# Decay attention feeding two gated MLPs: the order of the first weight loads, and where the state's decay is computed

## The chip, the cores and the metric

The kernel runs on one NeuronCore of a Trainium2 chip. The metric is device time in microseconds (us), the median of several executions. TensorE (PE) does the matrix products, VectorE (DVE), ScalarE (ACT) and GpSimd (POOL) the elementwise work, and SyncE (SP) issues every DMA, in program order, on one queue.

## The reference

Everything is float32: decayed linear attention with a running state, then two MLPs without a softmax or an activation table.

```
attention, batch 2, heads 8, sequence 768, head_dim 64, for each head with its decay lam:
    out_i = sum_{j<=i} lam^(i-j) (q_i . k_j) v_j        (written with blocks of 64 and a state kv)
x = out as 1536 tokens x 512
x = ((x @ w_a) * (x @ w_b)) @ w_out                      w_a, w_b: 512 x 1536
out = max(x @ w1, x @ w2, x @ w3) @ w_out2               w1, w2, w3: 512 x 768
```

## The kernel before, in words

The kernel uses blocks of 128 tokens (C = 128), so there are 6 blocks (`c`) for each of the 2 batches (`b`): twelve steps n = 0 to 11 in `order`. For step n, `load` brings queries and keys into the tile `aq` (issue L385, 512 KB) and keys and values into `av` (also 512 KB; columns 0 to 511 are keys, 512 to 1023 values). `scores` (L395) multiplies keys by queries into two PSUM banks, `masked` (L418, DVE, two instructions) applies the decay table and frees them, `side` (L405, L408, POOL) scales the queries and the keys for the state, and `values` (L434, L439, L446) takes two more banks `o`: scores by values, queries by state, and keys by values for the new state. After `values`, ACT copies the result into `x` (L190, two instructions), DVE adds the new state (L458 for the first block, L460 later), and multiplies it by the decay of a block into `stt` (L463, 128x256, for c < 4), which the next block of that batch adds.

PSUM has eight banks, handed out in turn by `bank`; a matmul into a bank waits until the earlier tile in it was read.

The weights come as float64 (`wup`, 1024 KB an item). `converted` turns an item into float32: L223 (DVE), L226 (ACT), L228 (DVE), L231 and L233 (ACT), L235 (DVE). Then `up_pair` splits it into a rounded part `hi` (ACT copy, L190) and the rest `lo` (DVE subtract, L187), since every product is done as three products of such parts. Raw items have two buffers (`wr`), so the load of item m + 2 waits until L228 of item m has read its own. In the code before, that load is issued straight behind L228 of item m (`load_to(m + 2)`, L229), and it stands in SP's queue ahead of what is issued later.

The attention output is split in the same manner (`Operands`: x0 for the first three blocks, x1 for the last three; `x0A` are its plain quarters A11, A12, A21, A22, and `x0S` their sums). From n = 7 on, one step of the first MLP (`plain_group`, L552, twelve matmuls into a bank `p`) follows each attention step. Items 0 and 1 serve those; from item 2 on `Group.product` (L534, tiles `zu`, `bu`, `xu`) takes over.

The order on DVE, ACT and POOL is fixed when the program is written, by the planner `Pace`. It keeps a model clock for each engine, advanced by a cost for each instruction; `pace.pe(cost)` moves PE's clock and then `pump` lets tasks (item conversions, operand splits) emit their next instruction if their input and their engine are free, by the model, within 2 us of PE's clock. Tasks with a lower rank come first. A task at a gate waits until the program opens it (`open_to`). On the chip every engine then works through its list strictly in that order, apart from PE's weight loads, and waits where an input is not there.

Of the kernel before, what the change touches and what calls it, by code (L numbers as in the profile page):

```python
# [12 lines left out]
AF = mybir.ActivationFunctionType  # L13
ALU = mybir.AluOpType

B, H, S, D = 2, 8, 768, 64
C = 128
NC = S // C
NP = H // 2
# [15 lines left out]
NPLAIN = 2  # L35
# [127 lines left out]
def decay_attention_gated_mlps(ctx: ExitStack, tc: tile.TileContext, qkv: bass.AP, lam: bass.AP, wup: bass.AP, wdown: bass.AP, out: bass.AP):  # L163
    nc = tc.nc
# [7 lines left out]
    pace = Pace()  # L172
# [27 lines left out]
    def load_to(n):  # L200
        while state["raw"] <= min(n, len(items) - 1):
            m = state["raw"]
            kind, i = items[m]
            t = wp.tile([128, 1024], I64, tag="r", bufs=2, name=f"wr{m}")
            if kind == "up":
                nc.sync.dma_start(out=t, in_=wup[i])
            else:
                nc.sync.dma_start(out=t[:, 0:WB], in_=wdown[i])
            raw[m] = t
            state["raw"] += 1  # L210

    def converted(m, width, roomy=False):

        load_to(m)
        bits = raw.pop(m)[:, 0:width].bitcast(I32).rearrange("p (n two) -> p n two", two=2)
        low, high = bits[:, :, 0], bits[:, :, 1]
        yield ("DVE",), width, "2"
        t = slot(f"wd{m}") if roomy else hp.tile([128, 1792], F32, tag="h", name=f"w{m}")  # L220
        f = t[:, 0:width]
        w = f.bitcast(I32)
        nc.vector.tensor_scalar(out=w, in0=high, scalar1=3, scalar2=0x40000000, op0=ALU.logical_shift_left, op1=ALU.bitwise_xor)  # L223
        yield ("ACT",), width + 60, "S"
        sign = wp.tile([128, width], F32, tag="s", bufs=1, name=f"ws{m}") if width > WB else t[:, WB:2 * WB]
        nc.scalar.activation(out=sign, in_=high.bitcast(F32), func=AF.Identity, bias=bias[:, 0:1])  # L226
        yield ("DVE",), width, "S"
        nc.vector.scalar_tensor_tensor(out=w, in0=low, scalar=29, in1=w, op0=ALU.logical_shift_right, op1=ALU.bitwise_or)  # L228
        load_to(m + 2)  # L229
        yield ("ACT",), width, "S"  # L230
        nc.scalar.activation(out=sign, in_=sign, func=AF.Sign, bias=bias[:, 1:2])  # L231
        yield ("ACT",), width, "S"
        nc.scalar.activation(out=f, in_=f, func=AF.Abs)  # L233
        yield ("DVE",), width, "S"
        nc.vector.tensor_tensor(out=f, in0=f, in1=sign, op=ALU.mult)  # L235
        return t

    wop, wtask = {}, {}
# [60 lines left out]
    def items_to(m):  # L299
        while state["item"] <= min(m, len(items) - 1):  # L300
            n = state["item"]
            kind, i = items[n]
            wtask[n] = pace.opens["done", n] = pace.add((up_pair if kind == "up" else down_block)(n, i), 1 if n > 1 else -1)
            state["item"] += 1

    def open_to(what, m):
        if m < len(items):
            items_to(m)
            pace.open((what, m))
# [20 lines left out]
    ltab = tables_sb[:, 1024:1536].rearrange("p (a i) -> p a i", a=NP)  # L330
# [31 lines left out]
    order = [(b, c) for c in range(NC) for b in range(B)]  # L362
# [14 lines left out]
    def load(n, *which):  # L377

        if n >= len(order):
            return  # L380
        b, c = order[n]
        for i in which:
            of, name = ((aq, "aq"), (av, "av"))[i]
            of[n] = slot(f"{name}{n}")
            nc.sync.dma_start(out=of[n][:, 0:1024], in_=qkv[b * NC + c, i])  # L385

    def scores(n):
        if n >= len(order):
            return
        q, k = aq[n][:, 0:512], aq[n][:, 512:1024]  # L390
        banks = [bank(f"s{n}_{g}") for g in range(2)]
        for h in range(H):
            r, p = rows(h), h // 2
            o = slice(128 * p, 128 * p + 128)
            nc.tensor.matmul(banks[side_of(h)][:, o], k[r, o], q[r, o], start=True, stop=True)  # L395
        sc[n] = banks
        pace.pe(1.1)
# [24 lines left out]
    def values(n):  # L422
        b, c = order[n]
        v, kd, qs = av[n][:, 512:1024], av[n][:, 1024:1536], aq[n][:, 1024:1536]
        ps = [bank(f"o{n}_{s}") for s in range(2)]

        def place(h):
            r, p = 64 * (h % 2), h // 2
            return ps[p % 2][r:r + 64, 128 * (p // 2):128 * (p // 2) + 128]

        for h in range(H):
            p = h // 2
            o = 512 * side_of(h) + 128 * p
            nc.tensor.matmul(place(h), v[:, 64 * h:64 * h + 64], am[n][:, o:o + 128], start=p < 2, stop=False, skip_group_check=True)  # L434
        pace.pe(1.1)
        if c > 0:
            for h in range(H):
                p = h // 2
                nc.tensor.matmul(place(h), sts[b][rows(h), 64 * p:64 * p + 64], qs[rows(h), 128 * p:128 * p + 128], start=False, stop=False, skip_group_check=True)  # L439
            pace.pe(0.65)  # L440
        kv = ps[1][:, 256:512]
        if c < NC - 1:
            for h in range(H):
                p = h // 2
                o = 256 * side_of(h) + 64 * p
                nc.tensor.matmul(kv[rows(h), 64 * p:64 * p + 64], kd[:, o:o + 64], v[:, 64 * h:64 * h + 64], start=False, stop=p == NP - 1, skip_group_check=True)  # L446
            pace.pe(0.65)
        j, r = c // 3, c % 3
        if r == 0:
            xa[j, b] = slot(f"x{j}{b}").rearrange("p (a i) -> p a i", a=KD)  # L450
        for s in range(2):
            copy(xa[j, b][:, s:KD:2, C * r:C * r + C], ps[s][:, 0:256].rearrange("p (a i) -> p a i", a=2))
            pace.run("ACT", 256)
        if c < NC - 1:
            src = kv.rearrange("p (a e) -> p a e", a=NP)
            std = sts[b].rearrange("p (a e) -> p a e", a=NP)
            if c == 0:
                nc.vector.tensor_copy(std, src)  # L458
            else:
                nc.vector.tensor_tensor(out=std, in0=src, in1=stt[b], op=ALU.add)  # L460
            pace.run("DVE", 256)
            if c < NC - 2:
                nc.vector.tensor_tensor(out=stt[b], in0=std, in1=ltab[:, :, C - 1:C].to_broadcast([128, NP, 64]), op=ALU.mult)  # L463
                pace.run("DVE", 256, kind="S")


    def split_part(a, h, l):
# [6 lines left out]
    class Operands:  # L474
# [5 lines left out]
        def __init__(self, a, name, order=ORDER):  # L480
            self.ops, self.name, self.made = {}, name, {}
            a11, a12, a21, a22 = a[0][:, 0:2], a[0][:, 2:4], a[1][:, 0:2], a[1][:, 2:4]
            s12 = slot(f"{name}s12").rearrange("p (s a n) -> p s a n", s=2, a=2)
            s1, s2 = s12[:, 0], s12[:, 1]
            self.sums = {"S1": (s1, a21, a22, ALU.add), "S2": (s2, s1, a11, ALU.subtract), "S3": (a21, a21, a11, ALU.subtract), "S4": (s1, a12, s2, ALU.subtract)}
            self.src = {"A11": a11, "S1": s1, "S2": s2, "A12": a12, "A21": a21, "S3": a21, "A22": a22, "S4": s1}
            self.tasks = {}
            for i, x in enumerate(order):
                t = self.tasks[x] = pace.add(self.make(i, x, "A21" in order), 0)
                for g in ("sum", "part"):  # L490
                    pace.opens[name, g, x] = t

# [201 lines left out]
    with tc.manual_schedule():  # L694
# [6 lines left out]
            nc.gpsimd.memset(bias[:, i:i + 1], (1 - 2 * i) * ROUND)  # L701
        nc.scalar.activation(out=warm[:, 0:1], in_=warm[:, 0:1], func=AF.Copy)
        ps = bank("warm_ps")
        for i in range(9):
            nc.tensor.matmul(ps, warm[:, 0:128], warm, start=True, stop=True)
        powers()
        load(0, 1)
        tables()
# [3 lines left out]
        load(3, 0)  # L712
        load(2, 1)
        pace.t["PE"] = 6.0
        for n in range(3):
            scores(n)
        pace.t["PE"] = 12.0
        for n in range(2):
            masked(n)
            side(n)  # L720
# [47 lines left out]
        for n in range(len(order)):  # L768
            load(n + 4, 0)
            load(n + 3, 1)  # L770
            if n in (1, 4):
                m = n // 4
                open_to("conv", m)
                open_to("split", m)
            if n == 7:
                open_to("conv", NPLAIN)
            if n > 0:
                scores(n + 2)
            side(n + 2)
            masked(n + 2)  # L780
            values(n)
            if n % 6 == 5:
                j = n // 6
                xo[j] = Operands([xa[j, b] for b in range(B)], f"x{j}", Operands.PLAIN)
                for i in range(8):
                    pace.open((f"x{j}", i))
            if n == 10:
                pace.open(("x0", "sums"))
            if n > 6:
                next(layer1)  # L790
# [116 lines left out]
```

## Time and profile before

| | |
|---|---|
| median of 3 runs | 546.04 us (545.58 to 546.85) |
| profiled execution | 545.02 us, its span 543.2 us |
| PE busy | 511.7 us (94%) |
| DVE busy | 377.4 us (69%) |
| ACT busy | 280.7 us (52%) |
| POOL busy | 48.2 us (9%) |
| mean granted TensorE clock | 0.984 |

The span is what the profiler saw of the engines; what lies around it makes the difference to the profiled execution's own time (1.8 us). Times in the rows count from the start of the span. Attention fills the first 70 us or so, the first MLP runs to about 346 us, the second to the end. A granted clock of 1.00 is 2.4 GHz, one of 0.50 is 1.2 GHz.

### The profile page before, as it was taken

The numbers are of one execution on the slowest core, as the hardware profiler recorded it, in microseconds if no ns is written. First come the engines' busy times: TensorE is split into PE (matmuls) and PEld (weight loads), VectorE is DVE, ScalarE is ACT, GpSimd is POOL, SyncE is SP. The second block draws the span as 40 slices with busy tenths as digits, with TensorE's granted clock in tenths as the row PEclk, the third lists the DMA queues.
The fourth block names the chain that finished last, engine by engine and source line by source line (L and its number), as shares of the span: only waits on it lengthen the run. The fifth ranks groups of instructions, "written<-read, shape, count | busy, mean of one in ns | idle before, by whom it ended". The sixth has DMA issues, their size and how long they took to land.

```text
span 543.2 us, 7761 instructions
## 1 busy us (share of the span) xinstructions
PE 511.7 (94%) x3167; PEld 469.3 (86%) x3167; DVE 377.4 (69%) x554; ACT 280.7 (52%) x419; POOL 48.2 (9%) x46
## 2 busy tenths in 40 slices
PE   4886999999999999999899999998999999978997
PEld 2765899999999999997678888798999999966886
DVE  3288888887777777489879069375898989892000
ACT  1163564765555555368887066535665566671111
POOL 1647000011111110111000000000000000000000
PEclk9888999999999999999999999999999999997999
DMA  7985310222222211015452001000222211200111
GB/s 223 406 346 209 122 74 1 78 77 78 78 78 78 77 60 58 2 59 174 151 197 78 1 0 43 36 1 0 78 78 77 80 58 59 83 34 39 59 70 66
DMA packets 11812, 48.49 MB, mean 89 GB/s; under 512 B 1272, under 2 KB 3072, under 8 KB 9088
## 3 DMA queue, kind: packets, MB, share of 16 engines
q1 hardware_dynamic: 11776, 47.99, 24.6%
q8 instruction: 25, 0.41, 0.3%
q14 instruction: 11, 0.09, 0.1%
HBM read 44.83 MB, written 3.15 MB: 88 GB/s over the span
## 4 chain that ended last, share of the span: by engine, by line
PE 77%; DVE 12%; DMA 5%; ACT 4%; issue 1%; SPq 1%; ACTq 0%
PE zu L534 15%; PE yp L657 13%; PE zv L534 11%; PE out L685 9%; PE bu L534 7%; PE p L552 7%; PE bv L534 6%; PE xu L534 4%; PE xv L534 2%; DMA aq<-qkv_dram 2%; DMA wr<-wup_dram 2%; DVE m L594 1%; PE o L434 1%; DVE wd L228 1%; DVE w L228 1%
## 5 line engine op out<-in xcount | busy, mean ns | idle before, releaser
L187 DVE TENSOR_TENSOR lo<-w,hi 128x1024 fp32r<-128x1024 f32 (+1 forms) x40 | 49.1, 1235 | 6.7 <-ACT hi L190 6.7
L190 ACT ACTIVATE hi<-w 128x1024 fp32r<-128x1024 f32 (+1 forms) x40 | 37.3, 953 | 13.3 <-DVE w L187 7.9
L657 PE MATMUL yp<-gh,dh 128*128 128x512 f32 x108 | 42.3, 391 | 1.9 <-ACT dh L190 1.9
L657 PE MATMUL yp<-gh,dl 128*128 128x512 f32 x108 | 42.2, 391 | 0.9 <-DVE dl L187 0.9
L657 PE MATMUL yp<-gl,dh 128*128 128x512 f32 x108 | 42.0, 389 | 0.0
L187 DVE TENSOR_TENSOR gl<-g,gh 128x512 fp32r<-128x512 f32 x36 | 24.7, 700 | 19.3 <-ACT gh L190 19.3
L583 POOL TENSOR_TENSOR g<-z1u,z6u 128x384 f32<-128x384 f32 x20 | 22.1, 1104 | 172.7 <-DVE z6u L565 116.6
L688 DVE COPY ob<-out 128x256 f32<-128x256 f32 x1 | 0.4, 425 | 47.6 <-PE out L685 47.6
L228 DVE SCALAR_TENSOR_TENSOR w<-wr,w 128x1024 int32<-128x1024 int32 (+1 forms) x26 | 31.1, 1196 | 0.5
L235 DVE TENSOR_TENSOR w<-w,ws 128x1024 f32<-128x1024 f32 x21 | 25.7, 1223 | 6.3 <-ACT w L233 6.2
L233 ACT ACTIVATE w<-w 128x1024 f32<-128x1024 f32 (+1 forms) x26 | 26.4, 1014 | 7.1 <-DVE w L228 6.9
L187 DVE TENSOR_TENSOR w<-w 128x256 f32<-128x256 f32 (+1 forms) x57 | 29.1, 510 | 1.2
L226 ACT ACTIVATE ws<-wr,bias 128x1024 f32<-128x1024 f32 x21 | 25.9, 1233 | 5.6 <-DMA wr<-wup_dram 5.6
L190 ACT ACTIVATE ob<-out 128x512 f32<-128x512 f32 (+1 forms) x12 | 7.0, 580 | 39.8 <-PE out L685 39.8
L657 PEld LDWEIGHTS yp<-gh,dh 128*128 128x128 f32 x108 | 20.3, 188 | 6.8 <-ACT dh L190 2.8
L190 ACT ACTIVATE z6u<-zu 128x384 f32<-128x384 f32 x20 | 9.8, 492 | 30.3 <-PE zu L534 30.3
L657 PEld LDWEIGHTS yp<-gh,dl 128*128 128x128 f32 x108 | 20.3, 188 | 6.0 <-DVE dl L187 1.8
L190 ACT ACTIVATE x<-o 128x256 f32<-128x256 f32 x24 | 8.9, 383 | 31.3 <-PE o L434 16.5
L231 ACT ACTIVATE ws<-ws,bias 128x1024 f32<-128x1024 f32 x21 | 24.1, 1148 | 0.3
L657 PEld LDWEIGHTS yp<-gl,dh 128*128 128x128 f32 x108 | 20.3, 188 | 4.1
L418 DVE TENSOR_TENSOR am<-s,tables 128x512 f32<-128x512 f32 x24 | 15.4, 682 | 10.4 <-DMA tables<-tab_d 6.4
L552 PE MATMUL p<-x0A,hi 128*128 128x384 f32 x64 | 18.4, 365 | 4.1 <-DVE x0A L187 4.1
(200 smaller groups left out, 1505.9 us busy)
## 6 DMA issues: line engine op xcount, KB each, us to landing
wr<-wup_dram SPq DMA_DIRECT2D x21, 1024.0 KB, 4.8
wr<-wdown_dram SPq DMA_DIRECT2D x12, 768.0 KB, 4.3
aq<-qkv_dram SPq DMA_DIRECT2D x12, 512.0 KB, 6.4
av<-qkv_dram SPq DMA_DIRECT2D x12, 512.0 KB, 8.5
out_dram<-ob SPq DMA_DIRECT2D x11, 256.0 KB, 2.0
tables<-tab_d SPq DMA_DIRECT2D x4, 128.0 KB, 4.0
tables<-tab_d SPq DMA_DIRECT2D x4, 64.0 KB, 4.4
out_dram<-ob SPq DMA_DIRECT2D x2, 128.0 KB, 1.7
```

Source lines behind the costliest of these rows:

```text
L187: (nc.vector if e == "DVE" else nc.gpsimd).tensor_tensor(out=o, in0=a, in1=b, op=op)
L190: nc.scalar.activation(out=o, in_=a, func=AF.Copy)
L226: nc.scalar.activation(out=sign, in_=high.bitcast(F32), func=AF.Identity, bias=bias[:, 0:1])
L228: nc.vector.scalar_tensor_tensor(out=w, in0=low, scalar=29, in1=w, op0=ALU.logical_shift_right, op1=ALU.bitwise_or)
L231: nc.scalar.activation(out=sign, in_=sign, func=AF.Sign, bias=bias[:, 1:2])
L233: nc.scalar.activation(out=f, in_=f, func=AF.Abs)
L235: nc.vector.tensor_tensor(out=f, in0=f, in1=sign, op=ALU.mult)
L534: nc.tensor.matmul(ps, w, x, start=p in FIRST and i == 0, stop=i == len(todo) - 1, skip_group_check=p not in FIRST)
L552: nc.tensor.matmul(ps, w[:, 128 * k:128 * k + 128], x[:, k], start=m == 0, stop=m == 11)
L583: nc.gpsimd.tensor_tensor(out=ga[g.n][:, tokens(g.j, 0)], in0=g.z[1], in1=g.z[6], op=ALU.mult)
L657: nc.tensor.matmul(ps[e], w[:, cols], g, start=k == 0 and m == 0, stop=k == K1 - 1 and m == 2)
L685: nc.tensor.matmul(ps, a[:, o:o + 128], w[:, s], start=k == 0 and n == 0, stop=k == K2 - 1 and n == 2)
```

## The change

- The loads of items 2 and 3 are no longer issued behind L228 of items 0 and 1, but at n = 9, behind every load of queries, keys and values. Item 0 is loaded and opened for conversion at n = 2 instead of n = 1, item 1 at n = 7 instead of n = 4 (before, its load was issued together with item 2's, behind L228 of item 0), item 2 is opened at n = 9 instead of n = 7.
- For the last block of each batch (c = 5, n = 10 and 11), `av` gets its values only: 256 KB in place of 512.
- The state's decay (L463) moves from DVE, one instruction of 128x256, to ACT, four of 128x64 with a scale for each partition: eight DVE instructions become 32 on ACT.
- `values(0)` is issued ahead of `scores(2)`; before, `scores(2)` stood ahead of the loop.
- Eight more empty matmuls (128x512, bf16, into the bank of the nine at the start) stand behind `scores(1)`.
- Ranks in the planner: item 1 from -1 to 1, item 2 from 1 to 0.5, the tasks of the sums S1 to S4 of x0 and x1 from 0 to 0.7. PE's model clock is set to 11 instead of 12 ahead of the first masks.

```diff
@@ converted
-        load_to(m + 2)
+        if m > 1:
+            load_to(m + 2)
@@ items_to
-            wtask[n] = ... 1 if n > 1 else -1)
+            wtask[n] = ... {0: -1, 2: 0.5}.get(n, 1))
@@ load
-            nc.sync.dma_start(out=of[n][:, 0:1024], in_=qkv[b * NC + c, i])
+            s = slice(512 if i == 1 and c == NC - 1 else 0, 1024)
+            nc.sync.dma_start(out=of[n][:, s], in_=qkv[b * NC + c, i, :, s])
@@ values
             if c < NC - 2:
-                nc.vector.tensor_tensor(out=stt[b], in0=std, in1=ltab[:, :, C - 1:C].to_broadcast([128, NP, 64]), op=ALU.mult)
-                pace.run("DVE", 256, kind="S")
+                for p in range(NP):
+                    nc.scalar.activation(out=stt[b][:, p], in_=std[:, p], func=AF.Copy, scale=ltab[:, p, C - 1:C])
+                    pace.run("ACT", 64)
@@ Operands
-                t = self.tasks[x] = pace.add(self.make(i, x, "A21" in order), 0)
+                t = self.tasks[x] = pace.add(self.make(i, x, "A21" in order), 0.7 if "A21" in order and x[0] == "S" else 0)
@@ ahead of the loop
-        for i in range(9):
-            nc.tensor.matmul(ps, warm[:, 0:128], warm, start=True, stop=True)
+        def keep_warm(n):
+            for i in range(n):
+                nc.tensor.matmul(ps, warm[:, 0:128], warm, start=True, stop=True)
+        keep_warm(9)
...
-        for n in range(3):
+        for n in range(2):
             scores(n)
-        pace.t["PE"] = 12.0
+        keep_warm(8)
+        pace.t["PE"] = 11.0
@@ the loop over n
-            if n in (1, 4):
+            if n in (2, 7):
                 m = n // 4
+                load_to(m)
                 open_to("conv", m)
                 open_to("split", m)
-            if n == 7:
+            if n == 9:
+                load_to(NPLAIN + 1)
                 open_to("conv", NPLAIN)
-            if n > 0:
-                scores(n + 2)
+            if n == 0:
+                values(n)
+            scores(n + 2)
             side(n + 2)
             masked(n + 2)
-            values(n)
+            if n > 0:
+                values(n)
```

## Rows read from the trace of the kernel before

**Rows 1.** Waits of PE from 0 to 72 us: total us, times, longest.
```profile
PE s L395 <- DMA aq<-qkv_dram: 7.0, 4, 4.9
PE p L552 <- DVE x0A L187: 4.1, 1, 4.1
PE o L434 <- DVE stt L458: 2.3, 1, 2.3
```

**Rows 2.** Busy time by stretch: PE, PEld, DVE, ACT, POOL, clock, DMA share, GB/s.
```profile
97.00:236.00 139.00, 139.00 (x803) 138.80 (x802) 105.40 (x151) 75.35 (x107) 19.40 (x18) 1.00 0.19 67
```

**Rows 3.** Timeline of SP's queue, 0 to 130 us: start, length, line, transfer.
```profile
15.86 0.46 SPq L206 DMA_DIRECT2D wr<-wup_dram  x1
...
21.81 11.53 SPq L206 DMA_DIRECT2D wr<-wup_dram  x2
```

**Rows 4.** Busy time by stretches of 2 us, columns as in rows 2.
```profile
28.00:30.00 2.00, 2.00 (x24) 1.67 (x28) 1.97 (x5) 0.62 (x3) 0.73 (x1) 0.50 1.05 420
...
32.00:34.00 2.00, 2.00 (x42) 1.54 (x40) 1.97 (x3) 1.85 (x2) 2.00 (x2) 1.00 0.40 127
```

**Rows 5.** The chain that ended last, 33 to 56 us: start, length, what.
```profile
33.38 6.00 DMA aq<-qkv_dram
...
51.11 3.92 PE p L552 x11
55.03 1.09 PE s L395 x16
```

**Rows 6.** Timeline of all engines, 18 to 30 us.
```profile
18.14 1.16 PE L395 MATMUL s<-aq 64*128 64x128 f32 x16 [0.34 <-DMA aq<-qkv_dram]
...
24.31 1.06 POOL L408 TENSOR_TENSOR av<-av,tables 128x512 f32<-128x512 f32 x1 [0.17 <-DMA av<-qkv_dram]
...
26.77 0.69 DVE L223 TENSOR_SCALAR w<-wr 128x1024 int32<-128x1024 int32 x1 [6.12 <-DMA wr<-wup_dram]
...
27.98 0.64 ACT L190 ACTIVATE x<-o 128x256 f32<-128x256 f32 x2
...
29.27 1.06 POOL L408 TENSOR_TENSOR av<-av,tables 128x512 f32<-128x512 f32 x1 [2.68 <-DMA av<-qkv_dram]
```

**Rows 7.** Groups by form, 0 to 60 us: busy us, mean ns, idle before.
```profile
L418 DVE TENSOR_TENSOR am<-s,tables 128x512 f32<-128x512 f32 x22 | 14.1, 682 | 10.4 <-DMA tables<-tab_d 6.4 <-PE s L395 4.1
L190 ACT ACTIVATE x<-o 128x256 f32<-128x256 f32 x18 | 6.8, 383 | 26.4 <-PE o L434 16.5 <-PE o L439 7.2 <-PE o L446 2.7
L463 DVE TENSOR_TENSOR stt<-stt,tables 128x256 f32<-128x256 f32 x8 | 5.2, 653 | 0.3
L190 ACT ACTIVATE x0A<-x 128x768 fp32r<-128x768 f32 x4 | 3.1, 832 | 0.0
L460 DVE TENSOR_TENSOR stt<-o,stt 128x256 f32<-128x256 f32 x7 | 2.9, 416 | 1.4 <-ACT x L190 1.3
L235 DVE TENSOR_TENSOR w<-w,ws 128x1024 f32<-128x1024 f32 x2 | 2.4, 1218 | 0.1
L228 DVE SCALAR_TENSOR_TENSOR w<-wr,w 128x1024 int32<-128x1024 int32 x2 | 2.4, 1216 | 0.0
L231 ACT ACTIVATE ws<-ws,bias 128x1024 f32<-128x1024 f32 x2 | 2.3, 1140 | 0.0
L187 DVE TENSOR_TENSOR lo<-w,hi 128x1024 fp32r<-128x1024 f32 x1 | 2.1, 2148 | 0.0
L190 ACT ACTIVATE hi<-w 128x1024 fp32r<-128x1024 f32 x2 | 2.1, 1053 | 0.0
```

**Rows 8.** Timeline of DVE, 54 to 62 us.
```profile
54.79 0.95 DVE L187 TENSOR_TENSOR x0A<-x,x0A 128x768 fp32r<-128x768 f32 x1
...
61.22 1.22 DVE L187 TENSOR_TENSOR lo<-w,hi 128x1024 fp32r<-128x1024 f32 x1
```

**Rows 9.** Timeline of DVE near 93 us.
```profile
93.37 1.22 DVE L187 TENSOR_TENSOR lo<-w,hi 128x1024 fp32r<-128x1024 f32 x1
```

**Rows 10.** The chain that ended last, near 97 us.
```profile
96.95 1.04 PE zu L534 x6
```

More of the change, by code (lines that the diff above doesn't have):

```diff
@@ L302, in items_to @@
             kind, i = items[n]
-            wtask[n] = pace.opens["done", n] = pace.add((up_pair if kind == "up" else down_block)(n, i), 1 if n > 1 else -1)
+            wtask[n] = pace.opens["done", n] = pace.add((up_pair if kind == "up" else down_block)(n, i), {0: -1, 2: 0.5}.get(n, 1))
             state["item"] += 1
```

## Prediction

> **What bounds the kernel now.** I read the busy time by stretches first. From 97 to 236 us PE is busy in every one of the 139 us at clock 1.00 [rows 2]; what can be won is ahead of that. The waits of PE in the first 72 us come next: 7.0 us for queries and keys (the longest, 4.9, for the third pair of the start), 4.1 for the first split operand `x0A`, 2.3 for a PSUM bank whose state DVE hadn't copied [rows 1]. Behind such waits the clock falls: the stretch 28 to 30 us, behind the 2.3, ran at 0.50 [rows 4], and the first plain products after the 4.1 took 3.92 us for eleven matmuls [rows 5], 0.356 each, against 1.04 for six, 0.173 each, at full clock [rows 10]: 2.0 us lost.
>
> Then the queue of SP. The first item's load, `wr0`, is issued at 15.86. At 21.81 SP comes to items 1 and 2; the latter's buffer is free only when L228 of item 0 has run, and SP stands for 11.53 us with all later queries and values behind it [rows 3]. The transfers drop to 127 GB/s in 32 to 34 us, from 420 [rows 4]. The eighth query load (aq8) is issued at 33.38 and lands 6.00 us later [rows 5].
>
> DVE is the second place. It sits idle 6.12 us for `wr0`, which lands at 26.77 [rows 6], because L223 was put ahead of the state copy that PE needs. The last line that matters is 55.03 in the chain: there the first twelve plain matmuls are done and scores(10) begin [rows 5]. From there on PE only works. So I price the change by where it puts this point.
>
> **The change, part by part.** *Loads.* SP no longer stops, so aq8 isn't late. But `wr0` now stands behind aq6 and av5 (opened at n = 2). The stream is full: av4 landed at 24.31, `wr0` (1024 KB) at 26.77, aq6 and av5 (1024 KB together) by 29.27 [rows 6], about 2.5 us each MB. With the two in front `wr0` lands at 29.3 and aq8, three loads of 1.25 us later, at 33.0. Item 1 lands behind ten more loads, near 44, item 2 near 47. The keys left out save 512 KB, 1.25 us of transfers at the stream's end, where nobody waits: zero; if all of it counted, -1.25. At n = 9 SP waits in front of item 3 for L228 of item 1; behind it stand only later weights.
>
> *The start.* Scores(3) began at 18.14, on the landing of its queries [rows 6]. All loads up to that one keep their order, so whatever PE does before, with values(0) first and eight empty matmuls in a wait of 4.9 us [rows 1], scores(3) can't begin earlier. If PE is slow for a while after 18.14, it still reaches scores(6) before its bank is free (below). I take zero for both edits; the ends are -1.2 (scores(3), 1.16 us [rows 6], starting one score earlier if loads come sooner) and +1.2 (one score more at half clock). If the cover of that wait were gone, each empty matmul would cost its own time.
>
> *What is late next: `wr0` on DVE.* I worked the planner's clocks through by hand with its costs (PE at 11, a mask (512+150)/960 = 0.69 and so on). DVE's list becomes: masks 2 and 3, state copy of n = 1, **L223**, masks 4, **L228**, add 2, masks 5, **L235**, add 3, masks 6, **lo** of item 0, add 4, masks 7, add 5, **lo A11**, masks 8, **lo A12**. ACT's: L226, x 2, decay 2, L231, L233, x 3, decay 3, hi of item 0, x 4, decay 4, x 5, decay 5, hi A11, hi A12. The stall for `wr0` stays. It no longer stops values(3), but it holds masks 4, hence scores(6). The new decays tie the two lists together: each waits for DVE's add and holds the conversion behind it on ACT, for which DVE then waits.
>
> A decay has no row. Four instructions of 64 columns: the copies of 256 take 0.383 alone, 0.64 for two in a row [rows 6, 7]; the slope to 768 columns (0.832) is 0.00088 a column, so 192 fewer save 0.17. Lower end: 0.21 + 3 x 0.09 = 0.48 for four. Upper end: no saving from the width and 0.09 for the scale operand, as L231 stands over the copy `hi` of the same width (1.140 to 1.053): 4 x 0.48 = 1.9 [rows 7]. I take 1.2, the middle.
>
> The Trainium skill (ScalarE: Activation LUTs, "What ACT_TABLE_LOAD costs") gives 186 ns plus 0.833 a column, 93 more for a pointer operand and 93 of overlap in a row, by which I estimate the four at 1.05; the sum would be 4 x 0.15 = 0.6 us shorter, 541.7. No trace here shows it yet.
>
> The sum from 29.3, durations from [rows 6 to 8]:
> - L223 0.69, masks 4 2 x 0.68, L228 1.22, add 0.42: 33.0
> - decay 1.2, L231 1.14, L233 1.05 (as `hi`, the same width): 36.4
> - L235 1.22, add 0.42: 38.0
> - decay 1.2, hi 1.05: 40.3
> - lo 1.22, add 0.42: 41.9
> - decay 1.2, x copies 0.64, decay 1.2, hi A11 0.83: 45.8
> - lo A11 0.95, masks 8 1.36, lo A12 0.95: 49.0
> - seven hand-overs between engines at 0.17 (the idle in front of the waiting POOL instruction at 24.31 [rows 6]): 50.2
> - the six matmuls with A12, 1.04 [rows 10]: **51.3**
>
> PE beside it: values(5) waits for add 3 (38.0) for its bank, scores(8) follow, values(6) wait for add 4 (41.9 and two hand-overs), then scores(9) and values(7). With values at about twice a score's 1.16, an estimate, PE is through at 48, ahead of A12. It idles for no more than some 2 us at a time there, so I take full clock at the product.
>
> Against 55.03 that is 3.7 us earlier. DVE loses its eight decays, 5.2 us busy [rows 7]; in this sum they are simply not there. The profiled execution would be 545.02 - 3.7 = 541.3; it lies 1.02 under the median of the runs, so the median goes from 546.04 to **542.3**.
>
> The ranks and gates I price at zero: item 1 is done, by the same lists, about 62, and its first product comes near 67; item 2 is done earlier than before. If that cover fails, it is the third rival.
>
> **Rivals.**
> *Wait not binding.* If ACT and DVE slip past each other (decays at 0.48, L233 early), DVE's own work is the floor: 0.69 + 5 x 1.36 + 1.22 + 4 x 0.42 + 1.22 + 1.22 + 1.9 = 14.7 from 29.3, or 44.0, and 45.1 with the product: 10 us earlier. Against it: hi of item 0 and L235 truly need each other's engine. Half way between it and my sum, 7 us, gives 539.
>
> *ACT's list as the bound: slower.* The mechanism: ACT works in order, and four decays stand between `wr0` and A12 with everything behind them. At 1.9 each they add 2.8. Beside that, DVE's subtracts stretch when POOL runs: `lo` took 2.15 in one place [rows 7], 1.22 in another [rows 8], 0.93 more. POOL is busy up to about 43 in the new order as well, with five such DVE instructions in the chain: 4.65 at most. It decides from 3.7 us of excess. All of it: 58.7, +3.7, 549.7; three fifths of the second with the first: 56.9, +1.9, 547.9. For it: DVE's masks 7 were done near 37 before and end near 43 in my lists. Against: before, the same stretch was paid at 45 to 51 by `lo` and `x0A`, which now come after POOL's work.
>
> The Trainium skill's "Rules for kernel authors" on that page puts multiplication on VectorE rather than ScalarE, which speaks for this rival; in the rows the DVE form took 0.65 [rows 7], and whether ACT's is longer no row shows.
>
> *Given back at item 2.* Its first `lo` ended at 93.37 + 1.22 = 94.6 [rows 9], its first product began at 96.95 [rows 10]: 2.4 us to spare. If the conversion, opened later, doesn't move up with PE, 1.3 of the 3.7 are lost again, 543.6, and with a microsecond for the later opening 544.6.
>
> *The change doesn't do what it says.* SP could stop at another wait, for a freed slot of the 26 in place of a weight buffer, and the bandwidth hole stays: 546.0.
>
> **How the numbers follow.** Forecast 0.50 (541 to 544), not binding 0.18 (537 to 541), given back 0.10 (543.6 to 545), no effect 0.07 (546), slower 0.15 (547.2 to 549.7). A measurement tells 0.2%, 1.1 us, from no change: 544.9 and 547.1. Faster: 0.50 + 0.18 + 0.07 of the given back, 0.75, and I take 0.72 for orders that I mis-worked; same 0.12; slower 0.16. For 8 in 10 the range leaves out the far end of the floor and most of the slower case: 538.3 to 547.2. The forecast's own range is 541 to 544.
>
> **What would show it.** Right: no wait of SP for L228 before all queries are issued; `wr0` landing near 29; DVE idle in front of L223 until then; ACT's decay waiting for L460 and L235 waiting for L233; the first product near 48 to 50 and scores(10) near 51. Wrong: scores(10) before 48 (the lists don't bind), or after 55 (slower), or PE waiting at the first `zu` (given back). The empty matmuls are wrong as costed if scores(3) moves by more than a microsecond from 18.1.

## The result: 4.6 us less, through the chain that was forecast

| | before | after |
|---|---|---|
| median of 4 runs | 546.44 us (545.58 to 547.06) | 541.83 us (541.26 to 542.30) |
| profiled execution, its span | 545.02, 543.2 us | 541.83, 540.1 us |
| scores(10) begin | 55.03 us | 50.90 us |
| DVE, ACT busy | 377.4, 280.7 us | 363.9, 285.2 us |

The ratio of after to before is 0.9916 [0.9898, 0.9934], faster by more than the measurement's 0.2%. The forecast was 542.3. Of the 13.5 us that DVE lost, the decays are only 5.2 [rows 7]; another 5.1 are the 21 `lo` of 128x1024, which took 1.50 each before and 1.25 after.

What PE waits for in the first 72 us of after (the columns of [rows 1]):

```profile
PE s L397 <- DVE am L420: 3.1, 1, 3.1
PE s L397 <- DMA aq<-qkv_dram: 2.6, 2, 1.4
...
PE o L436 <- DVE am L420: 1.7, 2, 1.0
PE o L436 <- DVE stt L462: 1.4, 2, 0.7
PE p L555 <- DVE am L420: 0.2, 1, 0.2
```

Against [rows 1], the waits for queries fell from 7.0 to 2.6 and the 4.1 for `x0A` is gone. In their place stands one wait of 3.1 for masks 4, which are behind L223, as the forecast said. Other small waits for masks and states came with it.

SP's queue in after, which answers to [rows 3]:

```profile
17.38 0.33 SPq L206 DMA_DIRECT2D wr<-wup_dram  x1
...
29.68 0.33 SPq L387 DMA_DIRECT2D av<-qkv_dram  x1
35.77 0.33 SPq L387 DMA_DIRECT2D aq<-qkv_dram  x1
...
41.12 81.46 SPq L206 DMA_DIRECT2D wr<-wup_dram  x6
```

The stop of 11.53 us at 21.81 is gone. The twelfth and last load of queries is issued at 35.77, after a stop of 5.7 for a slot (its releaser is the product `o`, L441), and the last load of values at 40.69, after one of 3.4. The next stop for L228 comes behind the issue at 41.12, with only weights behind it.

The chain that ended last, in after, from the landing of `wr0` to scores(10) (start, length, what; it answers to [rows 5]):

```profile
17.38 12.22 DMA wr<-wup_dram
29.63 0.69 DVE w L223
30.32 1.20 DVE am L420 x2
...
35.13 0.96 ACT w L234
36.11 0.57 DVE w L236
36.67 1.38 issue
38.05 0.42 DVE stt L462
38.50 1.07 ACT stt L466 x4
39.57 0.96 ACT hi L190
40.55 0.57 DVE lo L187
41.12 1.20 issue
42.31 0.42 DVE stt L462
42.76 1.07 ACT stt L466 x4
...
45.91 0.74 ACT x0A L190
...
48.39 2.51 PE p L555 x12
50.90 1.09 PE s L397 x16
```

Read it downwards: DVE and ACT take turns down to `x0A`, and each hand-over is one of the ties that the forecast named (the decay behind the add, L236 behind L234, `lo` behind `hi`). In the two stretches of "issue" behind L236 and `lo`, DVE was still at these two instructions; this is taken up below.

The lead stays. The last piece of the chain of waits, 222 `out` matmuls, begins at 491.76 before and 487.55 after, 4.21 earlier; it takes 48.48 before and 49.49 after. So 1.01 of the lead is lost within the same matmuls, and the two profiled spans differ by 3.1 only. The stretches show how (columns of [rows 2]), first of before, then of after:

```profile
480.00:490.00 10.00, 5.96 (x24) 4.15 (x24) 9.90 (x16) 6.82 (x9) 0.00 (x0) 0.92 0.00 0
490.00:500.00 10.00, 8.24 (x29) 6.41 (x30) 2.66 (x3) 2.04 (x3) 0.00 (x0) 0.74 0.07 26
```

```profile
480.00:490.00 10.00, 5.83 (x15) 3.54 (x14) 8.40 (x11) 5.19 (x7) 0.00 (x0) 0.65 0.00 0
490.00:500.00 10.00, 10.00 (x39) 8.13 (x38) 0.00 (x0) 1.20 (x2) 0.00 (x0) 0.84 0.14 52
```

PE waits twice there, in both kernels (2.3 us for `hl`, then 2.7 before and 1.9 after for `hd`). Before, the clock fell late in the first stretch; after, it was at half rate for more of it. In stretches of 2 us the clock before is 0.50 from 492 to 494 and 0.69 in the next, so it came back near 495.2, 3.5 us into the last chain; after, it is 0.50 from 490 to 492 and 0.70 in the next, so it came back near 493.2, 5.7 us into it. Half of these 2.2 us is about the 1.01. The profiles of the experiments with all 222 records have this chain at 48.4 to 49.1, and no run was made to separate what sets the clock there.

### The profile page after: what moved, and what is told of

The parts are those of the page before. It is cut to its first block, busy times and chain, and to the rows that moved or that the text cites. A ratio compares the mean times of both kernels' runs of the same rounds, so it can differ in the third digit from the quotient of the medians.

```text
span 540.1 us, 7792 instructions
## 1 busy us (share of the span) xinstructions
PE 513.7 (95%) x3175; PEld 470.1 (87%) x3175; DVE 363.9 (67%) x546; ACT 285.2 (53%) x451; POOL 50.2 (9%) x46
## 4 chain that ended last, share of the span: by engine, by line
PE 77%; DVE 11%; ACT 5%; DMA 4%; issue 2%; SPq 1%; ACTq 0%; DVEq 0%
PE zu L537 15%; PE yp L660 14%; PE zv L537 12%; PE out L688 9%; PE bu L537 7%; PE p L555 6%; PE bv L537 6%; PE xu L537 4%; PE xv L537 3%; DMA wr<-wup_dram 2%; DVE m L597 1%; DMA aq<-qkv_dram 1%; DVE wd L228 1%; DVE gl L187 1%; DVE w L228 1%
## 5 line engine op out<-in xcount | busy, mean ns | idle before, releaser
L187 DVE TENSOR_TENSOR lo<-w,hi 128x1024 fp32r<-128x1024 f32 (+1 forms) x40 | 44.2, 1109 | 12.5 <-ACT hi L190 12.5
L586 POOL TENSOR_TENSOR g<-z1u,z6u 128x384 f32<-128x384 f32 x20 | 25.1, 1257 | 172.8 <-DVE z6u L568 155.4
L236 DVE TENSOR_TENSOR w<-w,ws 128x1024 f32<-128x1024 f32 x21 | 26.5, 1262 | 15.1 <-ACT w L234 15.0
L228 DVE SCALAR_TENSOR_TENSOR w<-wr,w 128x1024 int32<-128x1024 int32 (+1 forms) x26 | 31.0, 1193 | 0.2
L234 ACT ACTIVATE w<-w 128x1024 f32<-128x1024 f32 (+1 forms) x26 | 26.3, 1013 | 6.9 <-DVE w L228 6.8
L190 ACT ACTIVATE z7u<-zu 128x384 f32<-128x384 f32 x20 | 9.8, 491 | 35.5 <-PE zu L537 35.4
L223 DVE TENSOR_SCALAR w<-wr 128x1024 int32<-128x1024 int32 (+1 forms) x26 | 17.5, 673 | 8.7 <-DMA wr<-wup_dram 8.7
L190 ACT ACTIVATE gh<-g 128x512 fp32r<-128x512 f32 x36 | 21.3, 622 | 1.6 <-PE yp L660 1.6
L568 DVE TENSOR_TENSOR z7u<-bu,z7u 128x384 f32<-128x384 f32 x20 | 11.1, 556 | 15.4 <-ACT z7u L190 15.4
```

The costliest lines, as they stand in the source:

```text
L187: (nc.vector if e == "DVE" else nc.gpsimd).tensor_tensor(out=o, in0=a, in1=b, op=op)
L190: nc.scalar.activation(out=o, in_=a, func=AF.Copy)
L586: nc.gpsimd.tensor_tensor(out=ga[g.n][:, tokens(g.j, 0)], in0=g.z[1], in1=g.z[6], op=ALU.mult)
```

## The experiments

Each is told by the start of scores(10) in its chain of waits, "the marker" (55.03 before, 50.90 after), and by its ratio to before. All kernels are after with one edit, except where it says before. A marker is from one profile, and the landing of item 0 ahead of it varies, by up to 0.74 in experiments 4 and 5, whose edits don't touch it.

**1. The loads undone (e1_old_loads).** Items 2 and 3 go behind L228 of items 0 and 1 again, item 1 ahead of item 2; the new openings stay.

```diff
-        if m > 1:
-            load_to(m + 2)
+        load_to(m + 2)
...
-                load_to(NPLAIN + 1)
```

> The changed kernel with one part undone: the loads of items 1 and 2 stand again behind L228 of item 0 (and item 3's behind L228 of item 1). The lists of DVE, ACT and PE stay as they are. Theory A (the point where scores(10) begin, 50.90 us, is set by a chain from the landing of item 0 through DVE and ACT): SP stops until L228 ends near 32.7, the queries of n = 7 land near 37 in place of 30, scores(7) come some 0.5 to 1 us late and the rest finds its loads nearly in time: scores(10) at 51.5 to 52.5, the time 1 to 2 us over the changed kernel's 541.8. Theory B (the stopped queue was the loss of before, 11.53 us of SP and 2 us of PE's direct waits behind it, and freeing it is the whole gain): scores(10) back near 55, the time 545.5 to 546.5.

Measured: marker 52.40, 542.84 us, ratio 0.9939 [0.9917, 0.9961]. Theory A holds, B (that the gain is the loads and nothing else) falls. SP's queue:

```profile
17.24 15.46 SPq L206 DMA_DIRECT2D wr<-wup_dram  x3
32.74 0.43 SPq L386 DMA_DIRECT2D aq<-qkv_dram  x1
```

The stop is back, 14.4 of these 15.46 us, and the queries behind it are late: scores(7) begin at 38.51 after a wait of 1.8, for 36.29 in after. (The row puts that wait down to a decay on ACT, which scores don't read. But scores(7) begin 5.8 us after the issue of their queries, and in experiment 3 again 5.8, 33.67 to 39.51, so it is taken for their landing here.) Still it costs only 1.5 at the marker, for DVE's chain doesn't move with it:

```profile
46.22 1.71 DVE L187 TENSOR_TENSOR x0A<-x,x0A 128x768 fp32r<-128x768 f32 x1 [1.86 <-ACT x0A L190]
...
50.05 0.62 PE L554 MATMUL p<-x0A,hi 128*128 128x384 f32 x2
```

`x0A` begins at 46.22, in after at 46.68; the first product comes straight behind PE's own late work.

**2. The decay on DVE again (e2_decay_on_vector).** L466 becomes one DVE instruction, the old L463.

```diff
-                for p in range(NP):
-                    nc.scalar.activation(out=stt[b][:, p], in_=std[:, p], func=AF.Copy, scale=ltab[:, p, C - 1:C])
-                    pace.run("ACT", 64)
+                nc.vector.tensor_tensor(out=stt[b], in0=std, in1=ltab[:, :, C - 1:C].to_broadcast([128, NP, 64]), op=ALU.mult)
+                pace.run("DVE", 256, kind="S")
```

> The changed kernel with the state's decay back on VectorE (eight instructions of 128x256). The planner then places lo of item 0 behind masks 8 and the lo of A11 and A12 behind add 7. Theory A: the ties of the two lists go (four decays of 1.07 us and their hand-overs leave the chain), but DVE's own list to lo A12 is 2 masks, 6 decays and 2 adds longer; from 29.6 it sums to about 50, the product then 51 to 52: 0 to 1.5 us slower than 541.8. Theory C (ScalarE's list is what binds, the decay there is a cost): scores(10) at 47 to 49, 2 to 4 us faster. Theory D (DVE's load was what the change relieved): all 5.2 us of decays come back, scores(10) at 55 or later, 545.5 to 547.

Measured: marker 52.80, 543.96 us, ratio 0.9953 [0.9936, 0.9970]. Theory A, that it is worse, was right, its size 0.8 too small at the marker and 0.7 in the time. DVE comes to `x0A` only at 48.67, PE waits 2.0 for it, and the clock falls (1.00 up to 50, 0.65 from 50 to 52, 0.50 from 52 to 54):

```profile
48.67 0.96 DVE x0A L187
49.67 3.13 PE p L554 x11
52.80 1.69 PE s L397 x16
```

**3. Both undone (e6_loads_and_decay_undone).** The edits of 1 and 2 together.

```diff
-        if m > 1:
-            load_to(m + 2)
+        load_to(m + 2)
...
-                    nc.scalar.activation(out=stt[b][:, p], in_=std[:, p], func=AF.Copy, scale=ltab[:, p, C - 1:C])
+                nc.vector.tensor_tensor(out=stt[b], in0=std, in1=ltab[:, :, C - 1:C].to_broadcast([128, NP, 64]), op=ALU.mult)
```

> The changed kernel with two parts undone together: loads of items 1 to 3 behind L228 as before, and the decay on VectorE. Alone they moved scores(10) by 1.5 (to 52.40) and 1.9 (to 52.80). If they cost in series: 54.3, 545 to 546, and only 0.7 us of the change's 4.1 at that point is left for the opening of item 0, the ranks and the rest. If they hide behind one another (the later of the two decides): 52.8 to 53.3, 544 to 545, and some 2 us belong to the rest.

Measured: marker 59.03, 549.09 us, ratio 1.0048 [1.0031, 1.0064]: slower than before. Both expectations are wrong. The edits cost 1.5 and 1.9 alone and 8.1 together.

DVE's timeline there (start, length, line, operation, tiles, then the idle time ahead):

```profile
44.93 0.42 DVE L461 TENSOR_TENSOR stt<-o,stt 128x256 f32<-128x256 f32 x1 [2.33 <-ACT x L190]
45.39 1.16 DVE L464 TENSOR_TENSOR stt<-stt,tables 128x256 f32<-128x256 f32 x1
...
53.08 3.75 DVE L187 TENSOR_TENSOR x0A<-x,x0A 128x768 fp32r<-128x768 f32 x3
```

The late queries hold the add at 44.93. In experiment 1 that add ran at 43.93 and `x0A` at 46.22, 2.3 later. Here 8.2 us lie between the two: three decays, two adds, masks and `lo`, since the planner, with the decays on DVE, put `x0A` behind them. And POOL's work, which the late queries hold up, now runs beside them: the three decays took 1.16, 1.05 and 0.86 for 0.43, `lo` 1.64 for 1.22, the first `x0A` 2.02 for 0.95 (the row has three in 3.75), 3.3 us more in all. In experiment 2 only the first of these decays was longer, 0.88. PE waited 3.6 for `x0A` and ran its first products at half rate (3.89 for eleven).

**4. The old start (e3_old_start).** Scores(2) ahead of the loop and values(0) behind scores(2), no empty matmuls behind scores(1); PE's model clock stays at 11.

```diff
-        for n in range(2):
+        for n in range(3):
             scores(n)
-        keep_warm(8)
...
-            if n == 0:
-                values(n)
-            scores(n + 2)
+            if n > 0:
+                scores(n + 2)
```

> The changed kernel with the start of before: scores(2) ahead of the loop and of values(0), no empty matmuls. Theory A: scores(3) and what follows wait for loads and then for item 0, which lands near 29.6 in both: scores(10) at 50.9 +- 0.3, the time within 0.5 us of 541.8. Rival (the start moves what follows): scores(2) and values(0) done some 2 us later and at half clock, and this carries through: scores(10) at 52.5 to 53, 543.5 to 544.

Measured: marker 50.56, 541.13 us, ratio 0.9908 [0.9881, 0.9934]. The start edits are worth nothing, as costed. PE waits once for 5.3 us for queries there, and scores(10) begin no later for it: the marker is 0.34 earlier, as L223 is 0.35 earlier (29.28 for 29.63).

**5. The full keys again (e11_full_keys).**

```diff
-            s = slice(512 if i == 1 and c == NC - 1 else 0, 1024)
-            nc.sync.dma_start(out=of[n][:, s], in_=qkv[b * NC + c, i, :, s])
+            nc.sync.dma_start(out=of[n][:, 0:1024], in_=qkv[b * NC + c, i])
```

> The changed kernel with the last block's keys loaded again (2 x 256 KB more). My costing: nobody waits at the stream's end, scores(10) at 50.9 +- 0.3, the time within 0.5 us of the changed kernel's. Rival: item 1, behind those loads, lands 0.6 us later and this carries through: scores(10) unchanged, the time 0.5 to 1.2 us longer.

Measured: marker 50.15, 542.15 us, ratio 0.9929 [0.9910, 0.9948]: in the time no difference to after that these runs can tell. The marker lies outside the expected 0.3, and not by the edit, whose loads stand far behind item 0: the item landed 0.74 earlier here, and the marker came 0.75 earlier.

```profile
28.89 0.69 DVE L223 TENSOR_SCALAR w<-wr 128x1024 int32<-128x1024 int32 x1 [7.61 <-DMA wr<-wup_dram]
```

**6. The old ranks (e7_old_ranks).** Item 1 at -1, item 2 at 1, the sums at 0.

```diff
-            wtask[n] = ... {0: -1, 2: 0.5}.get(n, 1))
+            wtask[n] = ... 1 if n > 1 else -1)
...
-                t = self.tasks[x] = pace.add(..., 0.7 if "A21" in order and x[0] == "S" else 0)
+                t = self.tasks[x] = pace.add(..., 0)
```

> The changed kernel with the planner's old ranks (items 0 and 1 at -1, the others 1, the sums 0). Up to masks 9 the lists of DVE and ACT are the same, so scores(10) stay at 50.9 +- 0.3. Behind that item 1 goes ahead of A21 and A22, and item 2's conversion comes last, behind all sums. Theory: PE then waits at the product with A22 or at the first products of item 2: 542.5 to 545. Rival (lists behind that point have spare time): 541 to 542.3.

Measured: 545.41 us, ratio 0.9986 [0.9972, 1.0000]. Nearly the whole gain is gone, 0.4 us beyond what was expected, though scores(10) begin at 50.71 (50.83 for after in the same view, PE's timeline). The last `out` chain begins at 491.03 for 487.55. Of these 3.5 us, PE's waits up to 110 us and the chain at item 2 show 2.5:

```profile
PE zu L537 <- DVE lo L187: 1.5, 1, 1.5
PE p L555 <- DVE x0A L187: 1.0, 1, 1.0
```

```profile
94.67 1.14 DVE lo L187
95.81 0.04 issue
95.86 0.98 PE zu L537 x4
```

In after, `lo` of item 2 is done 5.4 us ahead of its product:

```profile
86.03 1.23 DVE L187 TENSOR_TENSOR lo<-w,hi 128x1024 fp32r<-128x1024 f32 x1 [0.41 <-ACT hi L190]
...
92.65 0.51 PE L537 MATMUL zu<-x0A,hi 128*128 128x384 f32 x2
```

**7. Item 0 opened a step later (e4_open_at_3).** Its load stays at n = 2, so it lands as before, but L223 is planned behind masks 4.

```diff
             if n in (2, 7):
+                load_to(n // 4)
+            if n in (3, 7):
                 m = n // 4
-                load_to(m)
                 open_to("conv", m)
```

> The changed kernel with item 0 loaded where it is (n = 2) but opened for conversion at n = 3: L223 then stands behind masks 4 and add 2 instead of ahead of them, so DVE and PE do a pair's more work before the wait for item 0. Theory A (the stall of DVE for item 0 and the chain behind it bind): masks 4 and add 2 leave the chain, 1.7 us, and scores(6) and values(4) run during the wait; scores(10) at 45.5 to 48, the time 536.5 to 539. Theory B (the loads bind, queries and values or the freed slots they wait for): scores(10) within 1 us of 50.9, 541 to 542.5.

Measured: marker 46.70, 4.2 earlier than after, as theory A has it (0.6 of it by the landing, L223 at 29.04), but 540.83 us, ratio 0.9906 [0.9880, 0.9932], where 536.5 to 539 was expected. The last `out` chain begins only 1.5 earlier. Most of the 2.7 between is lost at item 3, in PE's waits from 90 to 110 us:

```profile
PE zu L537 <- ACT hi L190: 1.5, 1, 1.5
PE zu L537 <- DVE lo L187: 0.6, 1, 0.6
```

**8. The same with item 3 put ahead (e8_open_at_3_item_3_first).**

```diff
-            wtask[n] = ... {0: -1, 2: 0.5}.get(n, 1))
+            wtask[n] = ... {0: -1, 2: 0.5, 3: 0.6}.get(n, 1))
```

> The kernel with item 0 opened at n = 3, whose scores(10) began at 46.70, 4.2 us ahead of the changed kernel, but which lost 2.8 of it by 236 us, 2.2 in waits for hi and lo of item 3 at 102.6 and 103.9: here item 3 gets rank 0.6 instead of 1, ahead of the sums of x1. Theory A (the lead was given back at item 3's conversion): scores(10) at 46.7, no such wait, PE 4 us ahead of the changed kernel at 236 us, the time 537 to 538.5. Rival (another wait, for the sums of x1, takes its place): 540 to 541.5.

Measured: marker 46.29, 537.83 us, ratio 0.9837 [0.9817, 0.9858]. PE has no wait at `zu` up to 110 us, and the last `out` chain begins at 482.96, 4.6 before that of after, as the marker does: the loss of experiment 7 was that wait and what followed from it.

**9. Item 0 loaded a step earlier (e5_load_at_1).** Loaded at n = 1, opened at n = 2.

```diff
+            if n in (1, 7):
+                load_to(n // 4)
             if n in (2, 7):
                 m = n // 4
-                load_to(m)
```

> The changed kernel with item 0's load one pair earlier in SP's list (n = 1, as before the change), opened at n = 2 as in the changed kernel; no other instruction moves. Theory A (a chain from item 0's landing sets scores(10)): it lands about 2.5 us earlier, near 27.1, and scores(10) begin at 48.4 to 49.2 in place of 50.9; the time 539 to 540.5 if the later stages keep it. Theory B (queries and values, two of which now come 2.5 us later, bind as well): scores(10) at 50 to 51, 541 to 542.

Measured: L223 begins at 27.79 (29.63 after), the marker is 49.25, 540.15 us, ratio 0.9883 [0.9864, 0.9902]. A landing 1.84 earlier brings the marker 1.65 earlier: the landing is the head of the chain.

**10. Both of these (e12_load_at_1_open_at_3).** Loaded at n = 1, opened at n = 3, item 3 at 0.6: the version that the runs before it pointed to.

```diff
+            if n in (1, 7):
+                load_to(n // 4)
+            if n in (3, 7):
```

> Item 0 loaded at n = 1, opened at n = 3, item 3 at rank 0.6: the two steps that helped, together. In the kernel loaded at n = 2, DVE reached L223 near 28 to 29 and item 0 lands near 29.5, so little of the landing is still waited for. Theory A: item 0 landing 2.5 us earlier takes away what wait is left, at most 1 to 1.5 us; scores(10) at 45.3 to 46.3, 536 to 538. Rival (the two loads that item 0 overtakes are then waited for): scores(10) at 46.5 to 48, 538 to 539.5.

Measured: marker 45.96, 536.30 us, ratio 0.9828 [0.9810, 0.9846]: 9 us under before and the lowest median of all, though its interval overlaps that of experiment 8. The numbers are those of theory A, the chain is that of the rival: L223 begins 2.2 earlier than in experiment 8 (26.40 for 28.63), which gives only 0.3 at the marker. PE waits 1.6 us for the queries of scores(6), ahead of which item 0 now stands in SP's queue, and from there the chain of waits is PE's own work up to the marker, the first of it at half rate (2.00 for scores that take 1.16).

**11. Before with the loads alone (e9_before_loads_only).** Before, with items 1 to 3 loaded, and items 1 and 2 opened, as in after; up to item 2 DVE and ACT have the lists of before.

```diff
-        load_to(m + 2)
+        if m > 1:
+            load_to(m + 2)
...
-            if n in (1, 4):
+            if n == 7:
+                load_to(1)
+            if n in (1, 7):
...
-            if n == 7:
+            if n == 9:
+                load_to(NPLAIN + 1)
```

> The kernel before with one part done alone: the loads of items 1, 2 and 3 behind the queries and values (item 1 loaded and opened at n = 7, item 2 opened at n = 9), item 0 at n = 1 as before. The lists of DVE and ACT up to item 2 are those of before, word for word. Theory A (the stopped queue made scores(8) late, and with them masks 8, 9, lo and the splits, which then met POOL's late work): masks 8 follow masks 7 at once, scores(10) begin near 49.5 to 51 in place of 55.03; behind that the old ranks give some 1 to 2 us back, 541 to 543. Rival (undoing it cost 1.5 us in the changed kernel, so doing it alone gives 1.5): scores(10) at 53 to 54, 544.5 to 545.5.

Measured: marker 51.44, 543.03 us, ratio 0.9954 [0.9937, 0.9970]. It lies between the theories, nearer to A. The loads alone bring 3.6 at the marker. DVE no longer idles for scores(8) and their state (1.44 and 1.31 before), and POOL, no longer late, is done at 44.6: `lo` behind it takes 1.21 and the first two `x0A` 1.82, where before they took 2.15 and 3.96 beside it. Some DVE instructions ahead of 44.6 meet POOL here that didn't before (L236 2.12 for 1.21). PE still waits 4.1 for `x0A` and begins its products at half rate (3.89 for eleven).

**12. Before with the decay alone (e10_before_decay_only).**

```diff
-                nc.vector.tensor_tensor(out=stt[b], in0=std, in1=ltab[:, :, C - 1:C].to_broadcast([128, NP, 64]), op=ALU.mult)
-                pace.run("DVE", 256, kind="S")
+                for p in range(NP):
+                    nc.scalar.activation(out=stt[b][:, p], in_=std[:, p], func=AF.Copy, scale=ltab[:, p, C - 1:C])
+                    pace.run("ACT", 64)
```

> The kernel before with one part done alone: the state's decay on ScalarE. In the planner's list L223 then moves ahead of masks 3, and the conversion of items 0 and 1 ahead of masks 6 to 9 and of the splits. Theory A (the decay's move is worth what the planner makes of it; alone it puts conversions in front of what PE waits for): scores(10) at 54 to 58, 545 to 549. Rival (taking 5.2 us off VectorE helps by itself): scores(10) at 52 to 53.5, 543 to 545.

Measured: marker 58.06, 550.97 us, ratio 1.0097 [1.0079, 1.0114]. Theory A holds at the marker, at the upper end of its range; the time is 2 us above its range. The longest waits of PE up to 110 us:

```profile
PE p L553 <- DVE x0A L187: 6.3, 1, 6.3
PE s L395 <- DMA aq<-qkv_dram: 4.0, 1, 4.0
```

The products behind the 6.3 began at 54.14 and ran at half rate (3.92 for eleven). With DVE's model clock relieved, the planner puts the conversions of items 0 and 1 ahead, L223 even ahead of masks 3, and `x0A` comes last (all four in 6.38 from 52.48 on, beside POOL; 3.56 in experiment 2). An engine was relieved and the kernel became slower.

## Why the prediction was right, point by point

**The loads.** Right: no stop for L228 ahead of the last query, and `wr0` in time, 29.63 for 29.3 (L223's start; DVE idles 8.68 ahead of it, for 6.12 in [rows 6]). Without their delay the queries no longer hold PE more than 1.4 at a time. (The load at 33.38 in [rows 5], which the prediction calls the eighth, is the ninth, aq8.)

```profile
29.63 0.69 DVE L223 TENSOR_SCALAR w<-wr 128x1024 int32<-128x1024 int32 x1 [8.68 <-DMA wr<-wup_dram]
```

**The start and the keys at zero.** Right within what these runs can tell, by experiments 4 and 5. Scores(3) began at 17.41 for 18.14 [rows 6], inside the microsecond allowed.

**The sum.** Term by term, from the chain and DVE's timeline of after:

| done | forecast | measured |
|---|---|---|
| `wr0` landed | 29.3 | 29.6 |
| first add (n = 2) | 33.0 | 33.0 |
| L234 on ACT (was L233) | 36.4 | 36.1 |
| L236 and the second add | 38.0 | 38.5 |
| decay, `hi` | 40.3 | 40.5 |
| `lo` and the third add | 41.9 | 42.7 |
| `hi` of A11 | 45.8 | 46.6 |
| `lo` of A12 | 49.0 and 1.2 of hand-overs | 49.7 |
| scores(10) begin | 51.3 | 50.9 |

The order of the lists was as worked out by hand. That the sum ends within 0.4 us is in part luck: four terms were off and nearly cancelled.

*The decay* took 1.07 for four, not 1.2, so 0.5 us less for the four in the sum:

```profile
38.50 1.07 ACT L466 ACTIVATE stt<-stt,tables 128x64 f32<-128x64 f32 x4 [1.89 <-DVE stt L462]
```

By the figures of the Trainium skill (ScalarE: Activation LUTs, "What ACT_TABLE_LOAD costs") the prediction's estimate was 1.05, and this row agrees.

*DVE beside POOL* was left out of the sum and stands in only one rival. L236 took 2.02 for the 1.22 of [rows 7], `lo` 1.84 for 1.22: 1.4 us in all. DVE, then POOL:

```profile
36.11 2.02 DVE L236 TENSOR_TENSOR w<-w,ws 128x1024 f32<-128x1024 f32 x1 [1.93 <-ACT w L234]
...
40.55 1.84 DVE L187 TENSOR_TENSOR lo<-w,hi 128x1024 fp32r<-128x1024 f32 x1 [0.89 <-ACT hi L190]
```

```profile
35.78 1.27 POOL L407 TENSOR_TENSOR aq<-aq,tables 128x512 f32<-128x512 f32 x1
...
40.25 1.06 POOL L410 TENSOR_TENSOR av<-av,tables 128x512 f32<-128x512 f32 x1
```

Both DVE instructions began while a POOL instruction ran, which had 0.94 and 0.76 to go, and were 0.80 and 0.62 longer than alone. POOL waits for DVE in the same way: its L410 that began at 37.30, with 0.83 of L236 to go, took 1.75 for 1.06. Masks and adds, with one input in PSUM, kept their 0.68 and 0.42 beside POOL. In experiment 1, where POOL stood idle up to 39.69, L235 and `lo` (from 39.39) took 1.23 each; there `x0A` met POOL instead (1.71 for 0.95). The Trainium skill (SBUF — State Buffer, "SBUF: two separate sides") says that a DVE instruction with two SBUF inputs and a GpSimd instruction that reads SBUF exclude each other for a whole instruction, the one that starts first going first; the rows agree, but for 0.14 in each case.

*An add was left out.* Between the copies of `x` and the last decay stands the add of n = 5 (0.42 at 44.39): it waits for the copies, and the decay for it. The sum has only the adds of n = 2 to 4.

*The hand-overs* were counted twice. With the landing 0.3 later, POOL's 1.4, the add's 0.4 and four decays at 0.13 less the forecast's 49.0 becomes 50.6, and 49.7 was measured: there is no room for another 1.2 of hand-overs, and durations overlap besides. The decay of 1.07 at 38.50 ends at 39.57, and ACT's timeline has `hi` beginning at 39.48.

**PE beside it.** Right: scores(6) waited for masks 4 (3.1), values(5) and (6) for the adds (0.7 each), and PE was through at 48.2, for 48. The first products waited 0.2 for a bank that masks 8 had to free and ran at full clock, as taken (1.00 from 48 to 52): the twelve took 2.51 and the next twelve 2.28, and the 0.23 between is a wait of PE's weight load for `x0A` (`lo` of A12, done at 49.71). So A12 is the end of the chain as forecast, but by 0.2 only, with PE's own work close behind.

**What was mis-sized: the ranks at zero.** The prediction priced the ranks and gates at nothing, since item 2 had 2.4 us to spare. In after it has 5.4, and without the new ranks 1.5 are missing (experiment 6). They are worth 0.7% of the time, 3.8 us by the difference of the two ratios, nearly the size of the gain: the forecast counted on a cover that the change's own ranks provide. The price "given back at item 2" that the third rival named was too small for it: 544.6 at most, where 545.41 was measured. The rival didn't come about because the ranks were part of the change.

**What was not seen: the parts are not a sum.** The prediction counted one chain for the change as a whole, and that held. A reader who would price its parts by their lines finds -3.6 (loads alone, experiment 11) and +3.0 (decay alone, experiment 12) at the marker, from before, and +1.5, +1.9 and +8.1 (each and both undone, from after). In the order of before the decay on ACT costs, in that of after it pays, and more so with the old loads (8.1 less 1.5). Two things that the rows show make up the difference: where the planner puts `x0A`, and how much of POOL's work runs beside DVE's (3.3 us in experiment 3). The openings of items 0 to 2 and PE's model clock of 11 were not undone by themselves.

**The rivals.** *Not binding* falls: experiments 7 and 9 move the marker by moving L223, and the landings of experiments 4 and 5 do, so the chain bound; in experiment 10, with both, it no longer does. *ACT's list as the bound* falls for this order: the decays took less than 1.2, and POOL's 1.4 didn't come near its deciding point of 3.7. The decay is dearer on ACT, 1.07 for 0.42 on DVE alone (the 0.65 of [rows 7] is a mean, with POOL beside some), and the move still paid in this order (experiment 2). *No effect by a freed slot* was seen in part: SP did stop for one, 5.7 and 3.4 us, but only ahead of the last query and the last values, and no PE wait follows from it.

**The end.** The lead at scores(10) is 4.13, at the last `out` chain 4.21, so nothing in between gave it back. The profiled execution was forecast at 541.3 and took 541.83: the lead is 0.5 more than the 3.7 of the forecast, and the last stage gave 1.01 back, behind a clock that was longer at half rate. The medians differ by 4.6.

## What to carry to other kernels

Behind a relieved queue or engine look for the next late landing and for where its consumer stands in the in-order lists: here one step later in the list (experiment 7) was worth 3.6 us at the marker beyond its landing, and a landing 1.84 earlier (experiment 9) 1.65. When an early stage gets faster, move up by its rank what the later stage consumes first, or the lead ends in a wait there (experiments 6 to 8). Measure the parts of a change of order together as well as alone: parts of +1.5 and +1.9, each good to some 0.7 by the landing, made +8.1.

## What the runs showed of the hardware

Price a DVE instruction with both inputs in SBUF by what POOL still has to run when it starts: 2.02 and 1.84 us for 1.22 here, 0.83 for a decay of 0.43 in experiment 2 (0.54 of POOL to go). In each of the three the excess was the POOL instruction's remaining time less 0.14.

Nearly the same waits of PE were followed by different stretches at half rate: the last 222 `out` matmuls took 48.48 us in one profile and 49.49 in another, behind waits of 2.3 and 2.7 in the one and 2.3 and 1.9 in the other. A difference of one microsecond between two single profiles can be this, and one of 0.7 at an early marker the landing of a load: 29.63 and 28.89 for the same load in two profiles with the same list up to it.
